# Linear attention into two MLPs: a chunk's y stays on the chip, in 32-partition slots

## Chip, cores and metric

One core of a Trainium2 chip runs the whole program. The metric is device time in microseconds (us), as the median of several executions; engine names are those of the profile: PE (TensorE matmul), PEld (its weight loads), DVE (VectorE), ACT (ScalarE), POOL (GpSimd), SP (the queue that issues the DMAs).

## What is computed

A gated linear attention with 4 batches of 8 heads of 48, over 768 steps, then two MLPs over all 3072 tokens of 384 features (8 heads x 48). Cut to what matters:

```python
for t in range(S):                                    # S = 768, state is (B, H, 48, 48)
    state = alpha[:, :, t, :, None] * state + einsum('bhd,bhe->bhde', k[:, :, t], v[:, :, t])
    y[:, :, t] = einsum('bhd,bhde->bhe', q[:, :, t], state)
x = y.transpose(0, 2, 1, 3).reshape(B * S, H * D)     # 3072 x 384
h = x @ w1_in;  x1 = (h * sigmoid(1.702 * h)) @ w1_out   # 384 -> 2048 -> 384
h = x1 @ w2_in; out = (h - tanh(h)) @ w2_out
```

## The kernel before

**The MLPs.** Tokens go in six blocks of 512 per layer. A step is one block and one of 16 slices of d_ff: `gemm1` (L367) makes 128 rows of h with 9 matmuls 128x128x512, `gemm2` (L376) adds them into three accumulators with 9 more, three steps later (`LAG`). Each factor is split in a high and a low part (`whi`/`wlo`, `xhi`/`xlo`, `ghi`/`glo`), so a product costs three matmuls. The weights come as 64-bit words, and DVE and ACT convert them slice by slice with `conv` (L451: `w_bits`, `w_join`, `w_split`, L159 to L192), during the opening and the first token block.

**The attention.** It goes by chunks of 128 tokens, 24 of them (`g`), six to a batch (`c = g % 6`). Heads are taken in four pairs `p`: a pair's features lie on 112 partitions, head 0 on 0 to 47 and head 1 on 64 to 111. Per chunk: DVE scans the decays (`a_scan`, L241) and scales q and k (`a_scale`, L247 and L248; POOL does that from chunk 8 on). `a_scores` (L270) makes scores for two pairs at a time in banks b and b+1, ACT and POOL (DVE from chunk 8 on) copy and mask them into `sm`, and ACT copies the rest into `kts`. `a_out` (L293) then makes y in banks b and b+1 from two parts: `carried` (L306, 8 matmuls 48x48x128 from `state`, not for c = 0) and the part inside the chunk (L313, 8 matmuls 128x48x128 from v and `sm`); and the chunk's addition to the state (L322, 8 matmuls 128x48x48) in bank 7. `a_state` (L327) updates `state` on DVE (L333, L334, or L336 for c = 0). A matmul of plain fp32 is two instructions on PE in the profile, so 8 matmuls show as x16.

**From y to x.** `a_evac` (L338) copies y from the two banks to `ysb` on ACT (L341) and writes it to the DRAM tensor `xt` in four DMAs (L346). `a_back` (L356) reads it back into `xlo` with features in the order of x, on 128 partitions by 3 (L359). `a_x` (L361) rounds it into `xhi` on ACT (L363) and leaves the rest in `xlo` by a subtraction (L364: DVE for the first 8 chunks, POOL after).

**Order.** Chunks 0 to 3 run in an opening loop (L522 to L548), since the first token block needs all four. Chunks 4 to 7 run inside the steps of the first block, three steps each (`attend`, L484, with its parts r = 0 to 3). Up to the end of the first block every engine keeps the order of the program (`in_order`, L497). Chunks 8 to 23 run inside the steps of blocks 1 to 4, where a planner orders the instructions of each engine. In all places the queues are in order: what stands behind a waiting instruction waits too. In the first block the program has on DVE, per chunk g: `a_scale(g + 1)`, then `a_state(g)`, with three conversions of weights around them, and the first scores of chunk g + 1 (banks 5 and 6) come on PE after `a_out(g)`.

Of the kernel before, what the change touches and what calls it, by code (L numbers as in the profile page):

```python
# [68 lines left out]
def linear_attention_mlps(ctx, tc, xq, xv, fa, fv, cst, w1, w2, out):  # L69
# [30 lines left out]
    state = T("state", (DP, NP, D))  # L100
# [29 lines left out]
    ysb = [carve(NP * C), wtb[:, : NP * C]]  # L130
# [139 lines left out]
    def a_scores(g, x, b):  # L270
        u = (2 * g + x) % 2
# [20 lines left out]

    def a_out(g, b):  # L293
        c = g % NCH
        q = qq(g)
        y = [bank[b + hh][:, : 2 * C].rearrange("p (a t) -> p a t", a=2) for hh in range(2)]
        heads = [(p, hh) for a in range(2) for hh in range(2) for p in (2 * a, 2 * a + 1)]

        def at(p, hh):
            return y[hh][64 * (p % 2) : 64 * (p % 2) + D, p // 2]  # L300

        def carried(start):
            for p in range(NP):
                for hh in range(2):
                    r = slice(64 * hh, 64 * hh + D)
                    P.matmul(out=at(p, hh), lhsT=state[r, p], rhs=q[r, p, :C], start=start and p < 2, stop=not start and p >= 2)  # L306
# [4 lines left out]
        for p, hh in heads:  # L311
            s4 = sm[p // 2].rearrange("p (b a t) -> p b a t", b=2, a=2)
            P.matmul(out=at(p, hh), lhsT=vt(g)[:, p, D * hh : D * hh + D], rhs=s4[:, hh, p % 2],  # L313
                     start=(early or not c) and p < 2, stop=not (c and early) and p >= 2)
        if c and early:
            carried(False)
        if c < NCH - 1:
            dl = bank[7][:DP, : NP * D].rearrange("p (a e) -> p a e", a=NP)
            for p in range(NP):
                for hh in range(2):  # L320
                    kt = kts[p // 2].rearrange("p (b a d) -> p b a d", b=2, a=2)
                    P.matmul(out=dl[64 * hh : 64 * hh + D, p], lhsT=kt[:, hh, p % 2], rhs=vt(g)[:, p, D * hh : D * hh + D],  # L322
                             start=True, stop=True)
            if g >= FULL:
                a_state(g)

    def a_state(g):  # L327
        c = g % NCH
        if c < NCH - 1:
            dl = bank[7][:DP, : NP * D].rearrange("p (a e) -> p a e", a=NP)  # L330
            al = dec3(g + 1, 0)[:, :, C:].to_broadcast([DP, NP, D])
# [6 lines left out]
    def a_evac(g, b):  # L338
        ys = ysb[g % 2 if g < FULL else 0]
        for hh in range(2):  # L340
            A.copy(ys[:DP, 2 * C * hh : 2 * C * hh + 2 * C], bank[b + hh][:DP, : 2 * C])  # L341
        y4 = ys.rearrange("p (b a t) -> p b a t", b=2, a=2)
        tk = slice(g * C, g * C + C)
        for n in range(2):
            for hh in range(2):
                SP.dma_start(out=xt[2 * n + hh :: 4, :, tk].rearrange("h d t -> d h t"), in_=y4[64 * n : 64 * n + D, hh])  # L346
        if g >= FULL:
            a_back(g)
            a_x(g)


# [4 lines left out]
    def a_back(g):  # L356
        _, xl, o = a_at(g)
        tk = slice(g * C, g * C + C)
        SP.dma_start(out=xl[:, :, o].bitcast(F32), in_=xt.rearrange("h d t -> (h d) t")[:, tk].rearrange("(k p) t -> p k t", p=128))  # L359

    def a_x(g):  # L361
        xh, xl, o = a_at(g)
        A.copy(xh[:, :, o], xl[:, :, o].bitcast(F32))  # L363
        (V if g < FULL else G).tensor_tensor(out=xl[:, :, o], in0=xl[:, :, o].bitcast(F32), in1=xh[:, :, o].bitcast(F32), op=ALU.subtract)  # L364
# [112 lines left out]
    def a_done(g, b=5):  # L477
# [3 lines left out]
        if g < FULL:  # L481
            a_back(g)
# [32 lines left out]
    for b in (0, 1, 7):  # L515
        V.memset(bank[b], 0.0)
# [5 lines left out]
    for g in range(4):  # L522
# [12 lines left out]
        if g > 1:  # L535
            a_x(g - 2)
# [7 lines left out]
        if g:  # L544
            a_back(g - 1)
# [3 lines left out]
    a_back(3)  # L549
    conv(1)  # L550
    a_x(2)
# [194 lines left out]
```

## Time and profile before

| | |
|---|---|
| median of 3 runs | 960.14 us (960.0 to 963.54) |
| profiled execution | 956.15 us, of which the span is 954.1 us |
| PE busy | 920.1 us (96%), 4870 matmul instructions |
| DVE busy | 555.7 us (58%) |
| ACT busy | 462.6 us (48%) |
| POOL busy | 187.4 us (20%) |
| chain that ended last | PE 92%, DMA 2%, DVE 2%, ACT 1%, issue 1%, POOL 1% |

The span is cut by stage in what follows: the opening (to 46.5 us), the first steps (to 69 us), the rest of the first token block (to 134.3 us), blocks 1 to 4 with chunks 8 to 23 (to 460 us), and the rest without attention. "Busy" of PE is from records whose ends are modelled, so the distance from one start to the next tells more than the length of a row. A row of the timeline merges equal instructions that follow one another; the count stands at its end, and in square brackets the time that the engine had waited before it and for whom.

### The profile page before, as it was taken

To read this page: it belongs to the slowest core of one execution; us is meant where nothing else is said; L and a number is where in the kernel's file an instruction comes from. 1 tells how busy PE (TensorE), PEld (TensorE's weight loads), DVE (VectorE), ACT (ScalarE), POOL (GpSimd) and SP (SyncE) were. 2 spreads that over 40 slices of the span, in tenths; PEclk is the share of its full clock that TensorE was granted. 3 is DMA by queue.
4 is the path that set the end of the run, shared out by engine and by line. 5 is a ranking of instruction groups with operands and counts; after the bars stand their busy time and mean duration, and the time that the engine had idled before them with its cause. 6 is when DMAs were issued, how large, how long until landed. Compare 5 with 4: busy or idle time off the path is not lost.

```text
span 954.1 us, 13148 instructions
## 1 busy us (share of the span) xinstructions
PE 920.1 (96%) x4870; PEld 726.8 (76%) x4870; DVE 555.7 (58%) x820; ACT 462.6 (48%) x970; POOL 187.4 (20%) x150
## 2 busy tenths in 40 slices
PE   5579999999999999999999999999999999999997
PEld 4457777777777777777788888888888888888885
DVE  7899952231332332622059986766777777766663
ACT  4456534434344544433344564545656566544542
POOL 1101214444344444352400200100101001000000
PEclk9999999999999999999999999999999999999999
DMA  9867423341545534841235410200322430000001
GB/s 264 246 204 239 136 70 107 81 136 37 184 146 187 159 122 138 292 150 50 72 108 169 148 51 1 85 16 1 125 87 87 166 100 0 34 1 1 34 0 38
DMA packets 58041, 101.83 MB, mean 107 GB/s; under 512 B 4992, under 2 KB 37376, under 8 KB 57968
## 3 DMA queue, kind: packets, MB, share of 16 engines
q1 hardware_dynamic: 57968, 100.90, 33.4%
q8 instruction: 40, 0.66, 0.3%
q14 instruction: 33, 0.27, 0.1%
HBM read 86.73 MB, written 14.16 MB: 106 GB/s over the span
## 4 chain that ended last, share of the span: by engine, by line
PE 92%; DMA 2%; DVE 2%; ACT 1%; issue 1%; POOL 1%; SPq 0%; DVEq 0%; POOLq 0%; ACTq 0%
PE bank L380 42%; PE bank L373 41%; PE bank L277 4%; PE bank L313 3%; PE bank L306 1%; PE bank L322 1%; DMA arena<-xq 1%; DMA cs<-cst 1%; POOL arena L287 1%; DVE arena L241 0%; DMA xlo<-xt 0%; DVE wlo L192 0%; ACT whi L191 0%; ACT arena L282 0%; DVE xs L174 0%
## 5 line engine op out<-in xcount | busy, mean ns | idle before, releaser
L373 PE MATMUL bank<-xhi,whi 128*128 128x512 f32 x576 | 229.8, 399 | 8.3 <-ACT xhi L363 8.3
L380 PE MATMUL bank<-ghi,whi 128*128 128x512 f32 x576 | 230.5, 400 | 0.0
L373 PE MATMUL bank<-xlo,whi 128*128 128x512 f32 x576 | 229.6, 399 | 0.0
L373 PE MATMUL bank<-xhi,wlo 128*128 128x512 f32 x576 | 228.8, 397 | 0.0
L380 PE MATMUL bank<-ghi,wlo 128*128 128x512 f32 x576 | 228.1, 396 | 0.0
L380 PE MATMUL bank<-glo,whi 128*128 128x512 f32 x576 | 228.1, 397 | 0.0
L390 ACT CAST ghi<-gt 128x512 fp32r<-128x512 f32 x192 | 119.2, 621 | 186.1 <-DVE gt L402 130.6
L391 DVE TENSOR_TENSOR glo<-gt,ghi 128x512 fp32r<-128x512 f32 x128 | 93.1, 727 | 106.3 <-ACT ghi L390 102.7
L373 PEld LDWEIGHTS bank<-xhi,whi 128*128 128x128 f32 x576 | 109.1, 189 | 35.0 <-ACT xhi L363 8.4
L380 PEld LDWEIGHTS bank<-ghi,whi 128*128 128x128 f32 x576 | 108.7, 189 | 27.5 <-issue 2.9
L373 PEld LDWEIGHTS bank<-xlo,whi 128*128 128x128 f32 x576 | 109.1, 189 | 26.3 <-issue 1.0
L373 PEld LDWEIGHTS bank<-xhi,wlo 128*128 128x128 f32 x576 | 109.2, 190 | 25.4 <-issue 0.4
L380 PEld LDWEIGHTS bank<-glo,whi 128*128 128x128 f32 x576 | 108.7, 189 | 26.0 <-issue 0.8
L380 PEld LDWEIGHTS bank<-ghi,wlo 128*128 128x128 f32 x576 | 108.8, 189 | 24.6 <-issue 0.2
L391 POOL TENSOR_TENSOR glo<-gt,ghi 128x512 fp32r<-128x512 f32 x64 | 86.9, 1358 | 108.1 <-ACT ghi L390 82.4
L241 DVE TENSOR_TENSOR_SCAN arena<-arena,seg 112x516 f32<-112x516 f32 x46 | 66.4, 1444 | 50.3 <-DMA arena<-xq 31.4
L439 POOL TENSOR_TENSOR xlo<-arena,xhi 128x512 fp32r<-128x512 f32 x18 | 27.5, 1555 | 309.5 <-ACT xhi L438 309.5
L387 ACT ACTIVATE gt<-bank 128x512 f32<-128x512 f32 x96 | 57.5, 599 | 61.8 <-PE bank L373 57.2
L400 DVE SCALAR_TENSOR_TENSOR arena<-arena,bank 128x512 f32<-128x512 f32 x96 | 65.8, 685 | 30.1 <-ACT arena L398 29.3
L398 ACT ACTIVATE arena<-bank 128x512 f32<-128x512 f32 x96 | 57.3, 597 | 37.3 <-PE bank L373 36.9
L284 DVE TENSOR_TENSOR arena<-bank,cs 128x256 f32<-128x256 f32 x64 | 24.1, 416 | 86.9 <-PE bank L277 73.8
L402 DVE SCALAR_TENSOR_TENSOR gt<-arena 128x512 f32<-128x512 f32 x96 | 68.3, 712 | 10.2 <-DVE arena L401 0.5
(86 smaller groups left out, 785.3 us busy)
## 6 DMA issues: line engine op xcount, KB each, us to landing
raw<-w SPq DMA_DIRECT2D x64, 768.0 KB, 4.6
arena<-xq SPq DMA_DIRECT2D x46, 224.0 KB, 3.1
arena<-xq SPq DMA_DIRECT2D x22, 451.5 KB, 5.3
xlo<-xt SPq DMA_DIRECT2D x24, 192.0 KB, 4.3
x1t<-xs SPq DMA_DIRECT2D x6, 768.0 KB, 5.0
arena<-x1t SPq DMA_DIRECT2D x6, 768.0 KB, 4.5
out<-xs SPq DMA_DIRECT2D x18, 256.0 KB, 2.3
arena<-xv SPq DMA_DIRECT2D x23, 192.0 KB, 3.2
```

The lines of the kernel that those rows point to most:

```text
L241: V.tensor_tensor_scan(out=dec(g, n), data0=src(g, n), data1=seg, initial=0.0, op0=ALU.mult, op1=ALU.max)
L277: P.matmul(out=o[hh][:, i], lhsT=k[r, 2 * x + i], rhs=q[r, 2 * x + i], start=True, stop=True)
L313: P.matmul(out=at(p, hh), lhsT=vt(g)[:, p, D * hh : D * hh + D], rhs=s4[:, hh, p % 2], start=(early or not c) and p < 2, stop=not (c and e ...
L373: P.matmul(out=h, lhsT=w[m][:, ws], rhs=x[:, k, :n], start=c == 0, stop=c == 3 * KT - 1)
L380: P.matmul(out=acc[k][:, :n], lhsT=w[m][:, ws], rhs=x[s % 3][:, :n], start=m == 0 and c == 0, stop=m == MT - 1 and c == 2)
L387: A.activation(out=gf[i][:, :n], in_=h, func=AF.Silu, scale=1.702)
L390: A.copy(ghi[s % 3][:, :n], gf[s % 2][:, :n])
L391: e.tensor_tensor(out=glo[s % 3][:, :n], in0=gf[s % 2][:, :n], in1=ghi[s % 3][:, :n].bitcast(F32), op=ALU.subtract)
L398: A.activation(out=u, in_=h, func=AF.Square, accum_out=usum[:, s - NS1 :][:, :1])
L400: V.scalar_tensor_tensor(out=p, in0=u, scalar=P3, in1=h, op0=ALU.mult, op1=ALU.mult)
L402: V.scalar_tensor_tensor(out=gf[i], in0=w, scalar=PD, in1=p, op0=ALU.add, op1=ALU.mult)
L439: G.tensor_tensor(out=xlo[i][:, k], in0=xr[:, k], in1=xhi[i][:, k].bitcast(F32), op=ALU.subtract)
```

## The change

y is made where x has it. Features 0 to 383 of x lie in three groups k of 128 partitions; a pair of heads has 96 of them, that is three slots of 32: the first 32 of head 0, a shared slot (its last 16 and the first 16 of head 1), and the last 32 of head 1. Slot j = 3p + n lies in group j // 4 at partitions 32 (j % 4). One bank holds all twelve slots.

`state` becomes block-diagonal, 112 partitions by 96 columns a pair, and bank 7 likewise, set to zero once outside its blocks. `carried` has 12 matmuls of 112x32x128 in place of 8 of 48x48x128; the inner part has 16 of 128x32x128 in place of 8 of 128x48x128, since a shared slot takes one from either head, with v padded by zeros in the new tile `vmid`. `a_mid` fills `vmid` on ACT, two small copies a chunk. `a_state` works on twice as many columns. `a_evac` reads the bank twice, ACT into `xhi` and DVE for the subtraction into `xlo`, for all chunks. The DMAs to and from `xt`, the copies to `ysb`, `a_back` and `a_x` go; so does zeroing banks 0 and 1. The diff:

```diff
-    state = T("state", (DP, NP, D))
+    state = T("state", (DP, NP, 2 * D))
-    ysb = [carve(NP * C), wtb[:, : NP * C]]
+    vmid = [carve(H * 32).rearrange("p (a b e) -> p a b e", a=NP, b=2) for _ in range(2)]
...
     def a_scores(g, x, b):
+        if x == 0:
+            a_mid(g)
...
+    def a_mid(g):
+        v = src(g, 4).rearrange("p (a d) -> p a d", a=NP)[:, :, 32:64].rearrange("p a (b e) -> p a b e", b=2)
+        for hh in range(2):
+            A.copy(vmid[g % 2][:, :, hh, 16 * hh : 16 * hh + 16], v[:, :, hh])
+
     def a_out(g, b):
         c = g % NCH
         q = qq(g)
-        y = [bank[b + hh][:, : 2 * C].rearrange("p (a t) -> p a t", a=2) for hh in range(2)]
-        heads = [(p, hh) for a in range(2) for hh in range(2) for p in (2 * a, 2 * a + 1)]
-
-        def at(p, hh):
-            return y[hh][64 * (p % 2) : 64 * (p % 2) + D, p // 2]
+        y = bank[b][:, : KT * C].rearrange("p (k t) -> p k t", k=KT)
+        slots = [(k, [(j // 3, j % 3) for j in range(4 * k, 4 * k + 4)]) for k in range(KT)]
+
+        def at(p, n):
+            j = 3 * p + n
+            return y[32 * (j % 4) : 32 * (j % 4) + 32, j // 4]
 
         def carried(start):
-            for p in range(NP):
-                for hh in range(2):
-                    r = slice(64 * hh, 64 * hh + D)
-                    P.matmul(out=at(p, hh), lhsT=state[r, p], rhs=q[r, p, :C], start=start and p < 2, stop=not start and p >= 2)
+            for k, ps in slots:
+                for p, n in ps:
+                    P.matmul(out=at(p, n), lhsT=state[:, p, 32 * n : 32 * n + 32], rhs=q[:, p, :C],
+                             start=start and not k, stop=not start and k == 2)
+
+        def inner(start):
+            for k, ps in slots:
+                for p, n, hh in [(p, n, n // 2) for p, n in ps] + [(p, n, 1) for p, n in ps if n == 1]:
+                    s4 = sm[p // 2].rearrange("p (b a t) -> p b a t", b=2, a=2)
+                    w = vmid[g % 2][:, p, hh] if n == 1 else vt(g)[:, p, 32 * n : 32 * n + 32]
+                    P.matmul(out=at(p, n), lhsT=w, rhs=s4[:, hh, p % 2], start=start and not k and (n != 1 or not hh),
+                             stop=not (c and early) and k == 2 and (n != 1 or hh == 1))
 
         early = g < L1[0][1] // C
         if c and not early:
             carried(True)
-        for p, hh in heads:
-            s4 = sm[p // 2].rearrange("p (b a t) -> p b a t", b=2, a=2)
-            P.matmul(out=at(p, hh), lhsT=vt(g)[:, p, D * hh : D * hh + D], rhs=s4[:, hh, p % 2],
-                     start=(early or not c) and p < 2, stop=not (c and early) and p >= 2)
+        inner(early or not c)
         if c and early:
             carried(False)
...
-                    P.matmul(out=dl[64 * hh : 64 * hh + D, p], lhsT=kt[:, hh, p % 2], rhs=vt(g)[:, p, D * hh : D * hh + D],
-                             start=True, stop=True)
+                    r = slice(D * hh, D * hh + D)
+                    P.matmul(out=dl[64 * hh : 64 * hh + D, p, r], lhsT=kt[:, hh, p % 2], rhs=vt(g)[:, p, r], start=True, stop=True)
...
-            dl = bank[7][:DP, : NP * D].rearrange("p (a e) -> p a e", a=NP)
-            al = dec3(g + 1, 0)[:, :, C:].to_broadcast([DP, NP, D])
+            dl = bank[7][:DP, : 2 * NP * D].rearrange("p (a e) -> p a e", a=NP)
+            al = dec3(g + 1, 0)[:, :, C:].to_broadcast([DP, NP, 2 * D])
...
-    def a_evac(g, b):
-        ys = ysb[g % 2 if g < FULL else 0]
-        for hh in range(2):
-            A.copy(ys[:DP, 2 * C * hh : 2 * C * hh + 2 * C], bank[b + hh][:DP, : 2 * C])
...
-    def a_back(g):
...
-    def a_x(g):
+    def a_evac(g, b):
         xh, xl, o = a_at(g)
-        A.copy(xh[:, :, o], xl[:, :, o].bitcast(F32))
-        (V if g < FULL else G).tensor_tensor(out=xl[:, :, o], in0=xl[:, :, o].bitcast(F32), in1=xh[:, :, o].bitcast(F32), op=ALU.subtract)
+        y = bank[b][:, : KT * C].rearrange("p (k t) -> p k t", k=KT)
+        A.copy(xh[:, :, o], y)
+        V.tensor_tensor(out=xl[:, :, o], in0=y, in1=xh[:, :, o].bitcast(F32), op=ALU.subtract)
...
-    for b in (0, 1, 7):
-        V.memset(bank[b], 0.0)
+    V.memset(bank[7], 0.0)
+    for t in vmid:
+        G.memset(t, 0.0)
...
-        if g > 1:
-            a_x(g - 2)
...
-        if g:
-            a_back(g - 1)
...
-    a_back(3)
     conv(1)
-    a_x(2)
-    a_x(3)
...
-                if m % 3 == 1 and m > 3:
-                    a_x(m // 3 + 3)
```

## Rows read from the trace of the kernel before

**Rows 1.** The page: busy shares, and PE and DVE in 40 slices

```profile
PE 920.1 (96%) x4870; PEld 726.8 (76%) x4870; DVE 555.7 (58%) x820; ACT 462.6 (48%) x970; POOL 187.4 (20%) x150
...
PE   5579999999999999999999999999999999999997
...
DVE  7899952231332332622059986766777777766663
```

**Rows 2.** Windows by stage: us, busy of PE, PEld, DVE, ACT, POOL, clock, DMA, GB/s

```profile
46.40:69.00 22.60, 16.56 (x100) 11.79 (x100) 20.21 (x28) 11.77 (x25) 1.63 (x2) 1.00 0.67 198
69.00:134.30 65.30, 65.25 (x385) 50.90 (x386) 60.64 (x82) 34.00 (x76) 12.02 (x10) 0.97 0.58 176
134.30:460.00 325.70, 325.08 (x2047) 250.13 (x2046) 97.42 (x174) 136.96 (x304) 131.69 (x104) 1.00 0.42 131
```

**Rows 3.** Timeline, end of the opening: start us, us, engine line, count, [idle before]

```profile
36.30 1.11 PE L306 MATMUL bank<-arena,state 48*48 48x128 f32 x16
...
41.50 0.38 SPq L359 DMA_DIRECT2D xlo<-xt  x1
...
45.92 0.51 ACT L363 CAST xhi<-xlo 128x384 fp32r<-128x384 f32 x1 [2.75 <-DMA xlo<-xt]
...
46.47 0.56 DVE L364 TENSOR_TENSOR xlo<-xlo,xhi 128x384 fp32r<-128x384 f32 x1 [2.29 <-ACT xhi L363]
...
46.49 0.79 PE L373 MATMUL bank<-xhi,whi 128*128 128x512 f32 x1 [8.27 <-ACT xhi L363]
```

**Rows 4.** Timeline of DVE: its other longer waits between 20 and 69 us

```profile
22.83 0.36 DVE L333 TENSOR_TENSOR state<-bank,state 112x192 f32<-112x192 f32 x1 [1.04 <-PE bank L322]
...
32.47 0.96 DVE L192 TENSOR_TENSOR wlo<-cf,whi 128x768 fp32r<-128x768 f32 x1 [0.76 <-ACT whi L191]
...
53.64 0.96 DVE L192 TENSOR_TENSOR wlo<-xs,whi 128x768 fp32r<-128x768 f32 x1 [1.94 <-ACT whi L191]
```

**Rows 5.** Timeline: scores of chunks 5 and 7, and DVE's scaling before them

```profile
68.26 0.68 DVE L248 TENSOR_TENSOR arena<-arena 112x512 f32<-112x512 f32 x1
...
69.05 1.51 PE L277 MATMUL bank<-arena 48*128 48x176 f32 x8 [5.11 <-issue]
...
101.84 0.68 DVE L248 TENSOR_TENSOR arena<-arena 112x512 f32<-112x512 f32 x1
...
103.06 0.87 PE L277 MATMUL bank<-arena 48*128 48x176 f32 x8
```

**Rows 6.** Timeline of PE in very short windows: how many passes have started

```profile
59.62 0.33 PE L306 MATMUL bank<-arena,state 48*48 48x128 f32 x4
...
60.21 0.32 PE L313 MATMUL bank<-arena 128*48 128x128 f32 x2
...
251.35 0.42 PE L306 MATMUL bank<-arena,state 48*48 48x128 f32 x2 [0.58 <-ACT arena L290]
...
251.50 0.51 PE L306 MATMUL bank<-arena,state 48*48 48x128 f32 x5
```

**Rows 7.** Timeline of PE: carried and inner part of one later chunk

```profile
59.62 0.65 PE L306 MATMUL bank<-arena,state 48*48 48x128 f32 x16
60.21 1.08 PE L313 MATMUL bank<-arena 128*48 128x128 f32 x16
```

**Rows 8.** Groups by form: busy us, mean ns of one, idle before

```profile
L284 DVE TENSOR_TENSOR arena<-bank,cs 128x256 f32<-128x256 f32 x64 | 24.1, 416 | 86.9 <-PE bank L277 73.8 <-issue 8.8 <-ACT gt L387 4.0
...
L290 ACT COPY arena<-bank 128x96 f32<-128x96 f32 x96 | 21.6, 247 | 68.2 <-DVE arena L284 65.8
...
L333 DVE TENSOR_TENSOR state<-bank,state 112x192 f32<-112x192 f32 x16 | 5.7, 355 | 32.3 <-PE bank L322 32.3
...
L364 DVE TENSOR_TENSOR xlo<-xlo,xhi 128x384 fp32r<-128x384 f32 x8 | 4.3, 540 | 2.3 <-ACT xhi L363 2.3
```

**Rows 9.** Timeline of PE in the middle stage: end of a chunk, next scores

```profile
150.06 0.35 PE L322 MATMUL bank<-arena 128*48 128x48 f32 x8
...
154.72 0.87 PE L277 MATMUL bank<-arena 48*128 48x176 f32 x8
```

More of the change, by code (lines that the diff above doesn't have):

```diff
@@ L329, in a_state @@
         if c < NCH - 1:
-            dl = bank[7][:DP, : NP * D].rearrange("p (a e) -> p a e", a=NP)
-            al = dec3(g + 1, 0)[:, :, C:].to_broadcast([DP, NP, D])
+            dl = bank[7][:DP, : 2 * NP * D].rearrange("p (a e) -> p a e", a=NP)
+            al = dec3(g + 1, 0)[:, :, C:].to_broadcast([DP, NP, 2 * D])
             if c:
@@ L336, in a_state @@
                 V.tensor_tensor(out=state, in0=dl, in1=al, op=ALU.mult)
-    def a_evac(g, b):
-        ys = ysb[g % 2 if g < FULL else 0]
-        for hh in range(2):
-            A.copy(ys[:DP, 2 * C * hh : 2 * C * hh + 2 * C], bank[b + hh][:DP, : 2 * C])
[L342 to L349, printed above, removed]
     def a_at(g):
@@ L354, in a_at @@
         return xhi[j % 2], xlo[j % 2], slice(g * C - L1[j][0], g * C - L1[j][0] + C)
-    def a_back(g):
-        _, xl, o = a_at(g)
-        tk = slice(g * C, g * C + C)
-        SP.dma_start(out=xl[:, :, o].bitcast(F32), in_=xt.rearrange("h d t -> (h d) t")[:, tk].rearrange("(k p) t -> p k t", p=128))
-    def a_x(g):
+    def a_evac(g, b):
         xh, xl, o = a_at(g)
-        A.copy(xh[:, :, o], xl[:, :, o].bitcast(F32))
-        (V if g < FULL else G).tensor_tensor(out=xl[:, :, o], in0=xl[:, :, o].bitcast(F32), in1=xh[:, :, o].bitcast(F32), op=ALU.subtract)
+        y = bank[b][:, : KT * C].rearrange("p (k t) -> p k t", k=KT)
+        A.copy(xh[:, :, o], y)
+        V.tensor_tensor(out=xl[:, :, o], in0=y, in1=xh[:, :, o].bitcast(F32), op=ALU.subtract)
     def gemm1(i, m, h, n):
@@ L480, in a_done @@
             a_load(g + 2)
-        if g < FULL:
-            a_back(g)
     def attend(g, r, b=5):
```

## The prediction, made before the changed kernel was run

> **What bounds the kernel now.** I read the page's busy shares and its 40 slices first: PE is busy 96% and its digits are 9 from the fourth slice on, while DVE's are 7, 8 and then three times 9, that is up to 119 us, and low after them [rows 1]. The windows by stage say the same more sharply. From 69 to 134 us PE is busy 65.25 of 65.30 us and from 134 to 460 us 325.08 of 325.70, so there every PE instruction that is added lengthens the run by its own length. From 46.4 to 69 us it is different: PE is busy 16.56 of 22.60 us, DVE 20.21 [rows 2]. So there are two questions: what the change does to the path that ends at 69 us, and what it adds on PE after that.
>
> The round trip of y is seen at the end of the opening. PE's last carried part starts at 36.30, the read back from DRAM is issued at 41.50, ACT has waited 2.75 us when it rounds that chunk at 45.92, DVE has waited 2.29, and PE has stood still 8.27 us when the first gemm1 starts at 46.49 [rows 3]. That looks like 8 us to be had. But PE stops again, for 5.11 us, before the scores of chunk 5 at 69.05, and what it waits for is DVE's scaling that begins at 68.26 and lasts 0.68 [rows 5]. Between the two DVE waited once, 1.94 us [rows 4]. What PE gains at 46.49 it therefore loses again at 69.05, unless DVE's chain gets shorter. I cost the opening on DVE, not on PE.
>
> **PE, the size of a pass.** An fp32 matmul shows as two passes. At 251.35 the first head's matmul runs alone, because the next one waits for a bank: its two passes are the only two started until the window's end at 251.67; then, in the next 0.05 us, four passes of other heads start [rows 6]. So passes of one place in the array go one after another, and passes at different places go side by side, and a later matmul overtakes the waiting second pass of an earlier one. How many go abreast follows the shape: 48x48 (four places) starts four within 0.03 us, 128x48 (two places) starts two [rows 6]. The sixteen inner passes fill 60.21 to 61.12 less the hand-over, eight groups in 0.91, that is 0.114 us a group; the sixteen carried ones are four groups, 0.46, and 0.13 of the 0.59 to the next line is the switch to another shape [rows 7].
>
> The new matmuls have 32 columns and all rows, so four places. *Carried*: 12 matmuls, 24 passes, six groups in place of four: +0.23 us a chunk. *Inner*: 16 matmuls, 32 passes, eight groups if always four abreast, as many as now: +0. But its order isn't regular: the second matmul of a shared slot follows at once, and one place then gets two in turn while others wait. If a waiting matmul holds back all behind it, I count five rounds in place of four, ten groups: +0.23 us. I take eight, since [rows 6] show waiting passes overtaken, and keep ten for the range. The switch between carried and inner goes, one between inner and the state's part (L322) comes: nothing net.
>
> Here a rule of the Trainium skill speaks against the change. "TensorE: Matmul & The Clock Gate", Part 3, The mechanism, says that matmuls start and end strictly in program order. The trace disagrees for different places of the array: four carried passes within 0.03 us [rows 6] can't be in the order first, second, first, second. What it would cost if it came true is the third case below.
>
> **PE after 69 us.** Chunks 5 to 23 lie there; 16 of them have a carried part (6, 12 and 18 don't): 16 x 0.23 = +3.7 us, and the inner part 19 x (0 to 0.23) = 0 to +4.4. Chunk 4 falls into the stop before 69.05 and costs nothing as long as that stop is there.
>
> **DVE up to 69 us**, step by step, where + is later. In the opening a pass takes about twice as long: sixteen carried passes last 1.11 us at 36.30 and 0.65 at 59.62 [rows 3, 7]. Carried thus costs 0.46 a chunk, less about 0.2 for a switch that goes since L306 and L313 now share a shape: chunks 1 and 2 bring DVE's update of the state after chunk 2 +0.5, as it waits for PE (the like wait of chunk 1 is 1.04 in [rows 4]). The update handles 384 columns in place of 192: from 355 ns for 192 and 416 for 256 columns [rows 8], about 1 ns a column, I estimate 0.54, so +0.18 an operation and +0.36 a chunk. The subtraction for x now follows at once, from PSUM; SBUF took 540 ns for the same 384 columns, the slope above gives the same: 0.55. So after chunk 2: +0.5 +0.36 +0.55. The 0.76 wait that comes next [rows 4] is filled by that, and the subtraction of chunk 1, which stood before chunk 3's update, is gone (-0.54): about +0.1. Chunk 3's update and subtraction: +0.36 +0.55, so +1.0. Then what stood between the conversions goes: two subtractions and the 2.29 wait [rows 3], -3.4: DVE is 2.4 us early. The 1.94 wait stays: it comes from ACT's guard behind the scaling, and both only move. At the scaling of chunk 5 DVE is still 2.4 early, but then chunk 4's subtraction stands between it and the scores, which write the bank it reads: +0.55. PE resumes 1.8 us earlier. With ten groups chunks 0 to 2 cost 0.46 more each, 1.4 together, and 0.4 is left. What is late next is the same chain, DVE's conversions.
>
> After that DVE must keep up until the first block ends: before chunk 7's scores the scaling ends 0.54 us early (101.84 + 0.68 against 103.06) [rows 5]. DVE has 2.4 of gain and about 0.9 of new work (one update, one subtraction more), PE 1.8 of gain and 0.23 of new work: it still holds, barely.
>
> **What lies beside other work.** ACT loses two copies and one rounding that waits for a DMA, and gets one rounding from PSUM and two short copies, each at most like the 247 ns for 96 columns [rows 8]; ACT was busy 48% [rows 1]. POOL loses 16 subtractions and DVE gets them in a stage where it is busy 97 of 326 us [rows 2]. SP loses five DMAs a chunk, so loads behind them start earlier; no wait that PE feels hung on them. The new wait on PE in the middle stage is bank 5: next scores wait for ACT's rounding and then DVE's subtraction. From the end of a chunk at about 150.06 to the next scores at 154.72 there are 4.7 us [rows 9], and the two need 0.5 + 0.55 and at most one instruction ahead on each engine. I cost it at 0; if DVE is then held in a scan that waits for its load, PE stops behind it, with all that is queued: up to 1.5 us over the run for the range.
>
> **Sum.** -1.8 + 3.7 = +1.9 us on the profiled execution: 958.0. That execution is 956.15 (span 954.1), 3.99 below the median of 960.14. So the forecast is 962.0, by itself 959.5 to 964.5.
>
> **Rivals.**
> 1. *Ten groups in the inner part*, on PE. -0.4 + 3.7 + 4.4 = +7.7, so 967.8. For it: nothing in the trace shows an irregular order, and a waiting matmul may hold back those behind it. Against it: the overtaking in [rows 6]. It takes the time past 0.5% from the point where one of the two groups a chunk is lost: 19 x 0.114 = 2.2 and 0.7 at the start, +4.8 in all.
> 2. *Only two abreast*, the place is PE again: if four moving streams through all rows don't go, or order is strict. Carried 12 groups for 4 and inner 16 for 8, +0.91 each: 16 x 1.82 + 3 x 0.91 = 31.9, and about 7 in the opening: 999. Against it: four abreast is shown for two places by two, though with 48 of 128 rows each. By the page's rule on order named above it is this case.
> 3. *DVE doesn't hold the first steps*: then the 8.27 and the 5.11 both go [rows 3, 5], less 0.8 for the opening's passes: -13.4 + 0.8 + 3.7 = -8.9, so 951.2. Against it: DVE busy 20.21 of 22.60 us [rows 2].
> That the change doesn't do what it says (the DMAs stay, or the wait) I see no way for.
>
> **Chances.** Forecast 50%, ten groups 34%, two abreast 6%, rival 3 5%, and 5% for a new order of the planner in the middle stage, worth 1 or 2 us either way. The range goes from the forecast's own low end less 1 to rival 1 plus the stops of bank 5: 958.5 to 969.5. A difference over 0.5% (4.8 us) is about what a measurement of this kernel can tell from no change: below 955.3 only rival 3, 5%; above 964.9 most of ten groups, two abreast and a little of the forecast, 42%; the rest, 53%, within.
>
> **What would show it.** Carried as x24 over about 0.68 us and inner as x32 over 0.91 (right) or 1.14 (rival 1), and four starts within 0.03 us; a first gemm1 some 4 us earlier, but a longer stop before chunk 5's scores, ended by DVE's subtraction at 66.5 to 69; PE without stops after it. I would be wrong if that stop has gone, if scores wait at bank 5 in the middle stage, or if the carried and inner groups together take over 2.5 us.

## The result and the profile after

The changed kernel takes 972.52 us (median of 4 runs, 972.0 to 973.65), the kernel before 960.11 beside it: ratio 1.0131, 95% interval 1.0114 to 1.0149. That is slower by 12.4 us, outside the range of 958.5 to 969.5. The profiled execution of after took 972.51 (span 970.8), which is its median; that of before took 956.15, 4 us under its own. So between the two traces there are 16.4 us, and they are what the rows below have to explain.

The page of after, busy shares and the 40 slices of PE and DVE (against [rows 1]), and the windows by stage with the columns of [rows 2]:

```profile
PE 932.0 (96%) x5414; PEld 733.6 (76%) x5414; DVE 568.4 (59%) x834; ACT 455.0 (47%) x970; POOL 172.7 (18%) x136
...
PE   4479999999999999999999999999999999999997
...
DVE  7999852331242332632039986766777777766663
```

```profile
46.40:69.00 22.60, 13.27 (x119) 10.07 (x121) 20.41 (x29) 11.41 (x26) 2.03 (x2) 0.83 0.74 233
69.00:134.00 65.00, 65.00 (x441) 50.50 (x440) 58.39 (x78) 32.28 (x76) 11.46 (x10) 0.96 0.50 145
134.00:460.00 326.00, 326.00 (x2310) 250.59 (x2309) 108.61 (x186) 127.85 (x291) 112.50 (x86) 1.00 0.35 112
```

The shares tell nothing: PE 96% before, 96% after. The clock column of the first window needs care: before shows 1.00 there [rows 2] and after 0.83, but the trace of before has no clock record ahead of 55.5 us, and up to then its gemm1 matmuls start 0.43 us apart, behind that 0.23. In the windows PE is busy without a gap from 69 to 460 us. So the time isn't in a wait; PE has more to do, or does it more slowly. How much, and where, the ends of the blocks tell. DVE copies one third of each finished block of tokens out of PSUM; here the first of these twelve copies, the fifth (the last block that has attention beside it) and the last, first before, then after (timeline of DVE):

```profile
148.68 0.69 DVE L423 TENSOR_SCALAR xs<-bank 128x512 f32<-128x512 f32 x1 [4.36 <-PE bank L380]
...
483.80 0.69 DVE L423 TENSOR_SCALAR xs<-bank 128x512 f32<-128x512 f32 x1 [2.26 <-PE bank L380]
...
947.15 0.69 DVE L423 TENSOR_SCALAR xs<-bank 128x512 f32<-128x512 f32 x1 [1.90 <-PE bank L380]
```

```profile
149.80 0.69 DVE L421 TENSOR_SCALAR xs<-bank 128x512 f32<-128x512 f32 x1 [4.35 <-PE bank L378]
...
498.68 0.69 DVE L421 TENSOR_SCALAR xs<-bank 128x512 f32<-128x512 f32 x1 [2.28 <-PE bank L378]
...
963.90 0.69 DVE L421 TENSOR_SCALAR xs<-bank 128x512 f32<-128x512 f32 x1 [1.91 <-PE bank L378]
```

After is 1.1 us late at the first, 14.9 at the fifth and 16.75 at the last. The loss arises between 150 and 500 us, where the attention of the later chunks is slipped between the matmuls of the first MLP, and 1.9 us come in the seven blocks behind it, which hold no attention and which the change doesn't touch. The timeline of PE in that stage shows what it is (against [rows 7, 9]); the first fence is before and holds the start that follows the scores of [rows 9], the second is after, the third ACT and DVE of after beside it:

```profile
155.52 0.50 PE L373 MATMUL bank<-xhi,whi 128*128 128x512 f32 x1
```

```profile
149.70 0.86 PE L315 MATMUL bank<-arena,state 112*32 112x128 f32 x24
150.38 1.08 PE L323 MATMUL bank<-arena 128*32 128x128 f32 x32
151.39 0.39 PE L338 MATMUL bank<-arena 128*48 128x48 f32 x8
151.70 0.86 PE L280 MATMUL bank<-arena 48*128 48x176 f32 x4
152.50 0.50 PE L378 MATMUL bank<-ghi,whi 128*128 128x512 f32 x1
...
157.58 0.86 PE L280 MATMUL bank<-arena 48*128 48x176 f32 x4
158.37 0.50 PE L371 MATMUL bank<-xhi,whi 128*128 128x512 f32 x1
...
160.44 0.86 PE L280 MATMUL bank<-arena 48*128 48x176 f32 x4
161.23 0.50 PE L371 MATMUL bank<-xhi,wlo 128*128 128x512 f32 x1
```

```profile
151.52 0.48 ACT L361 CAST xhi<-bank 128x384 fp32r<-128x384 f32 x1 [1.82 <-PE bank L323]
...
152.30 0.55 DVE L362 TENSOR_TENSOR xlo<-bank,xhi 128x384 fp32r<-128x384 f32 x1
```

The new matmuls go as forecast: carried, 24 passes, 0.68 us to the next line; inner, 32 passes, 1.01. But the scores (L280), which the change doesn't touch, now stand as **x4** where [rows 9] have **x8**, and four passes take as long as eight: 151.70 to 152.50, 0.80 us; 157.58 to 158.37, 0.79; in the kernel before, 154.72 to 155.52 with eight, 0.80. A group of scores is four matmuls, two into bank 5 (heads in partitions 0 to 47) and two into bank 6 (partitions 64 to 111). When the four follow each other, one of each bank goes side by side: in the kernel before the passes from 154.72 on start in twos (154.72, 154.73; 154.98, 154.98), in the changed kernel one by one (151.70, 151.96, 152.11, 152.26). The planner now issues the two of one bank apart from the two of the other, with other matmuls between them, and two of the same partitions go one after the other. That the half at 151.70 is bank 6's follows from ACT and DVE, which read y out of bank 5 until 152.85.

Counted in the trace after 75 us, where there are 37 groups (a sum is the time from the first start of a group to the next matmul of another kind):

| us on PE after 75 us | before | after |
|---|---|---|
| scores | 31.2 | 41.8 |
| whole groups, halved (4+4), cut (2+6) | 34, 1, 2 | 21, 15, 1 |
| carried, inner, dl | 10.0, 17.7, 8.6 | 10.9, 19.3, 9.2 |
| changes from MLP to attention matmuls | 59 | 65 |

Scores +10.6 us (14 more halved groups at 0.79 more are 11.1, one cut less about -0.5), carried, inner and dl +3.0, six more changes of shape at about 0.1 on the way in and 0.1 on the way out (0.33 and 0.34 to the next start in place of 0.23) +1.2, less the stop of 0.58 at 251.35 that only the kernel before has [rows 6], and what the opening leaves, +0.6 at the second score group of chunk 5 (76.43 for 75.80): 14.8 of the 14.9 at the fifth copy.

The end of the opening (against [rows 3 to 5]), timeline of after, and behind it the scores of chunk 4 in the kernel before:

```profile
41.05 0.49 PE L371 MATMUL bank<-xhi,whi 128*128 128x512 f32 x1
...
50.41 1.54 PE L280 MATMUL bank<-arena 48*128 48x176 f32 x8 [5.48 <-DVE arena L249]
...
52.30 0.96 DVE L193 TENSOR_TENSOR wlo<-xs,whi 128x768 fp32r<-128x768 f32 x1 [1.94 <-ACT whi L192]
...
67.04 0.68 DVE L249 TENSOR_TENSOR arena<-arena 112x512 f32<-112x512 f32 x1
...
67.64 0.55 DVE L362 TENSOR_TENSOR xlo<-bank,xhi 128x384 fp32r<-128x384 f32 x1
...
68.25 1.54 PE L280 MATMUL bank<-arena 48*128 48x176 f32 x8 [5.32 <-DVE xlo L362]
```

```profile
51.75 1.54 PE L277 MATMUL bank<-arena 48*128 48x176 f32 x8 [0.89 <-DVE arena L248]
```

The first gemm1 starts 5.4 us earlier, and PE loses most of it already before chunk 4's scores: there it stands for 5.48 us in place of 0.89, until DVE's scaling is done, and starts only 1.3 us earlier (50.41 for 51.75). Before chunk 5's scores it stands for 5.32 us in place of 5.11, until DVE's scaling and then its subtraction for x are done; 0.8 us is left. Behind that stop the granted clock is at the lower level (1.2 of 2.4 GHz) for 6.8 us; in the kernel before it was for 3.4. Windows of after, then of before, the columns as above:

```profile
68.00:74.80 6.80, 6.55 (x20) 5.11 (x21) 6.65 (x12) 3.81 (x9) 1.31 (x1) 0.50 0.94 277
```

```profile
69.10:72.50 3.40, 3.40 (x13) 2.63 (x14) 3.33 (x6) 1.93 (x6) 0.97 (x1) 0.50 1.05 336
```

That is why the 0.8 us that PE is early at 68.25 are 0.6 late at 76.43.

### The profile page after: what moved, and what is told of

It is laid out like the page before. It is cut to its first block, busy times and chain, and to the rows that moved or that the text cites. A ratio compares the mean times of both kernels' runs of the same rounds, so it can differ in the third digit from the quotient of the medians.

```text
span 970.8 us, 14011 instructions
## 1 busy us (share of the span) xinstructions
PE 932.0 (96%) x5414; PEld 733.6 (76%) x5414; DVE 568.4 (59%) x834; ACT 455.0 (47%) x970; POOL 172.7 (18%) x136
## 4 chain that ended last, share of the span: by engine, by line
PE 93%; DVE 4%; DMA 1%; issue 1%; POOL 0%; ACT 0%; SPq 0%; ACTq 0%; POOLq 0%
PE bank L378 42%; PE bank L371 41%; PE bank L280 5%; PE bank L323 2%; PE bank L315 1%; PE bank L338 1%; DMA arena<-xv 1%; DVE wlo L193 0%; POOL arena L290 0%; DVE arena L242 0%; DVE cf L175 0%; DVE cf L162 0%; DVE cf L163 0%; DVE xlo L362 0%; DVE xs L163 0%
## 5 line engine op out<-in xcount | busy, mean ns | idle before, releaser
L385 ACT ACTIVATE gt<-bank 128x512 f32<-128x512 f32 x96 | 57.8, 602 | 74.7 <-PE bank L371 66.5
L242 DVE TENSOR_TENSOR_SCAN arena<-arena,seg 112x516 f32<-112x516 f32 x46 | 64.4, 1401 | 38.2 <-DMA arena<-xq 36.3
L280 PE MATMUL bank<-arena 48*128 48x176 f32 x368 | 55.5, 351 | 22.8 <-DVE arena L249 8.8
```

The lines of the kernel that those rows point to most:

```text
L242: V.tensor_tensor_scan(out=dec(g, n), data0=src(g, n), data1=seg, initial=0.0, op0=ALU.mult, op1=ALU.max)
L280: P.matmul(out=o[hh][:, i], lhsT=k[r, 2 * x + i], rhs=q[r, 2 * x + i], start=True, stop=True)
L385: A.activation(out=gf[i][:, :n], in_=h, func=AF.Silu, scale=1.702)
```

## The experiments

Two theories were to be told apart for the 10.6 us: the scores cost more because they stand apart (A), or the larger state, the new dependences and the new places of y cost it in some way that the scores only show (B). Beside that stood the prediction's reading of the opening, that DVE sets the end of the stop. All ratios are against the kernel before on the same chip.

| run | whole, halved, cut | scores us | median us | ratio, 95% interval |
|---|---|---|---|---|
| after | 21, 15, 1 | 41.8 | 972.52 | 1.0131 (1.0114 to 1.0149) |
| e1_pairs | 28, 0, 8 | 33.3 | 966.54 | 1.0074 (1.0045 to 1.0103) |
| e5_line | 31, 0, 6 | 32.6 | 963.32 | 1.0047 (1.0022 to 1.0072) |
| e6_scan_late | 32, 0, 5 | 31.9 | 961.47 | 1.0019 (1.0004 to 1.0034) |
| e10_two_banks | 30, 7, 0 | 35.1 | 965.78 | 1.0056 (1.0034 to 1.0078) |
| e2_before_banks | 30, 7, 0 | 35.2 | 963.22 | 1.0028 (1.0013 to 1.0043) |
| e12_before_held | 32, 1, 4 | 31.9 | 962.31 | 1.0014 (0.9995 to 1.0033) |

(One or two groups are missing from some traces.)

### The four score matmuls kept together

```diff
+        last = None
         for i in range(2):
             for hh in range(2):
-                P.matmul(out=o[hh][:, i], ...)
+                mm = P.matmul(out=o[hh][:, i], ...)
+                if last is not None:
+                    tc.add_manual_dep(mm.ins, last.ins.name, NoSync, reason="pairs")
+                last = mm
```

> The changed kernel, with the four score matmuls of two pairs chained in issue order (bank 5, 6, 5, 6), so that the planner can't issue bank 6's two alone. Theory A (split scores): in the changed kernel 30 halves of score groups stand alone and take 0.79 us each, as long as a whole group (0.80), so 15 groups cost 0.79 more and a switch of shape more. Whole again, scores fall from 41.8 us to about 31 and the run to 960 to 962. Theory B (bank 5): the planner only filled a wait for DVE's subtraction on bank 5; with the chain PE stops there instead and the run stays at 968 to 972. Theory C (the new 32-column matmuls or the clock): scores don't matter, 971 to 973.

Measured: 966.54, between the times of A (960 to 962) and B (968 to 972); 6.0 of the 12.4 us are back with an edit that only orders instructions on PE. The scores fell by 8.5 us, which the larger state and the new dependences can't give, as they are still there. But more than the 0.79 of a half hides in the rest: eight groups are still cut after the first matmul, dl is cut five times (11.15 us for 9.18), and there is a new stop. Timeline of DVE and PE of e1_pairs:

```profile
419.85 2.24 DVE L242 TENSOR_TENSOR_SCAN arena<-arena,seg 112x516 f32<-112x516 f32 x1 [8.99 <-DMA arena<-xq]
422.12 0.18 DVE L244 RECIPROCAL seg<-arena 112x4 f32<-112x4 f32 x1
422.22 0.39 DVE L292 TENSOR_TENSOR arena<-bank,cs 128x256 f32<-128x256 f32 x1
```

```profile
420.82 0.39 PE L383 MATMUL bank<-ghi,wlo 128*128 128x512 f32 x1
422.94 0.56 PE L281 MATMUL bank<-arena 48*128 48x176 f32 x2 [1.73 <-ACT arena L298]
423.43 0.29 PE L343 MATMUL bank<-arena 128*48 128x48 f32 x2
424.39 1.54 PE L281 MATMUL bank<-arena 48*128 48x176 f32 x6 [0.67 <-ACT arena L298]
```

```profile
424.10:431.00 6.90, 6.61 (x23) 5.18 (x24) 0.85 (x2) 2.35 (x6) 3.44 (x3) 0.51 0.12 33
```

DVE waits 8.99 us for the load of its next scan; the mask (L292) is queued behind that scan, though its scores had been made from 415.04 on, ACT's copy stands behind the mask, the next scores behind the copy. PE stops for 1.73 and 0.67 us, and then the granted clock is 0.51 for 6.9 us. The prediction had named such a stop, DVE "held in a scan that waits for its load", at up to 1.5 us, but with the subtraction for x held by it; here that was done at 410.39 and it is the mask.

### The price of a half, in the kernel before

```diff
-        for i in range(2):
-            for hh in range(2):
+        last = None
+        for hh in range(2):
+            for i in range(2):
```

The matmuls are chained as in e1_pairs, but in the order bank 5, 5, 6, 6.

> The kernel before, with the scores' order changed alone: both matmuls of bank 5, then both of bank 6, chained. Theory A, if a waiting pass is overtaken by one at another place: groups that stay together still take 0.80 us, those which the planner parts by other work cost 0.6 to 0.8 more each; 960 to 968 by how many are parted. If nothing is overtaken, the passes of one bank go one after another and every group takes about 1.4 us: 38 x 0.6 = 23 more, 983. Theories B and C: 960 (nothing but order is changed).

Timeline of PE:

```profile
154.95 0.87 PE L278 MATMUL bank<-arena 48*128 48x176 f32 x8
155.75 0.50 PE L385 MATMUL bank<-ghi,whi 128*128 128x512 f32 x1
...
160.61 0.86 PE L278 MATMUL bank<-arena 48*128 48x176 f32 x4
161.40 0.29 PE L327 MATMUL bank<-arena 128*48 128x48 f32 x2
161.62 0.86 PE L278 MATMUL bank<-arena 48*128 48x176 f32 x4
162.41 0.38 PE L327 MATMUL bank<-arena 128*48 128x48 f32 x6
```

As long as the four stand together the order does no harm: the group at 154.95 still takes 0.80 us, so the matmuls of bank 6 overtake the waiting second one of bank 5. Only where the planner put other work between the halves, seven times, do they cost 0.79 each: scores +4.0 us. With nothing of the change in it, the kernel before gets slower, by 3.4 us in the medians and 2.7 by the ratio. Not all of that need be the parting: dl is cut six times here too (9.9 us for 8.6), and this trace has the slower of two paces in the blocks without attention (last section).

The Trainium skill says the same from the other side ("TensorE: Matmul & The Clock Gate", section Why this matters for your kernels): small-K matmuls run concurrently when each lands in a distinct row group. The trace agrees: two of one bank share their partitions, 0.40 us each; one of each bank, 0.20 each.

### All attention matmuls in program order, and the scan behind the masks

e5_line: every matmul of scores, carried, inner and dl is chained behind the one before it; the MLP's may still come between. e6_scan_late: the same, and

```diff
+        if g > FULL:
+            tc.add_manual_dep(sc.ins, masked[0], NoSync, reason="scan")
...
-        if r == 0:
-            prep(g + 1, 0)
         if r < 2:
             a_scores(g, r, b)
+        if r == 0:
+            prep(g + 1, 0)
```

> Change: the kernel after, with all of PE's attention matmuls (scores, carried, inner, dl) held in program order among themselves, scores in the order bank 5, 6, 5, 6. Then neither dl nor the other half stands between the two banks' scores; 6 of about 38 groups are still parted by a gemm, one matmul from three. Theory A (the loss is scores that stand apart): the scores after 75 us fall from 41.8 us to about 32.5 and dl from 9.2 to about 8, so against the kernel after 10 to 11 us less on PE; if the stop near 420 us that the version with paired scores had comes again, 965 to 967, and without it 960 to 962. Rival B (the scores' order isn't what costs, the larger state and the new dependences do): no less than the 966.5 of the version with paired scores, whatever scores and dl sum to.

> Change: the kernel of the run e5_line, and DVE's first scan of a chunk from chunk 9 on stands behind the masks of the chunk before it. Theory: the stop near 420 us in the version with paired scores is masks that stand behind a scan which waits for its load; then no PE wait for ACT's copies and no low granted clock lies between 415 and 432 us, and the time is 4 to 6 us under a kernel that has that stop: 960 to 962. Rival: the scan only comes later and the scaling behind it becomes what PE waits for: the stop moves a few us, the clock falls as before, 965 to 967.

Measured: 963.32 and 961.47. e5_line has the stop near 420 again, shorter (2.11 us, then a clock of 0.50 for 3.4 us), and lies between the two times expected. In e6_scan_late it is gone; the windows of the same stretch:

```profile
415.00:424.00 9.00, 8.73 (x40) 6.44 (x39) 2.70 (x6) 3.28 (x10) 3.90 (x4) 1.00 0.43 128
424.00:432.00 8.00, 8.00 (x98) 6.40 (x97) 1.49 (x3) 3.63 (x8) 2.44 (x2) 1.00 0.21 55
```

PE is busy 16.73 of 17 us and the clock is 1.00; a stop of 0.74 us comes at 409.24, where PE waits for DVE's copy of a finished block, without a fall of the clock. The gain over e5_line, 1.9 us, is less than the 4 to 6 that were expected: e5_line's stop was the short one, and in the two profiled executions e6_scan_late has the slower of the two paces (1.9 us, last section). With whole scores and without the stop the changed kernel is at 961.5, and 11 of the 12.4 us are accounted for by two orders of instructions. That this is near the forecast (962.0) is in part luck: 1.8 us of it come from dl in one piece (7.4 us for 9.2), which the forecast didn't have.

### The held order in the kernel before

> Change: the kernel before, with all of PE's attention matmuls held in program order among themselves, scores in the order bank 6, 5, 6, 5 (35 of 41 score groups of four then stand whole, as 37 of 41 in the kernel before). A control: what the held order itself does. Theory A: the kernel before loses nothing in its scores, so there is nothing to regain: 957 to 963. Rival: the held order is good in itself (fewer switches, dl in one piece): 1 to 3 us less, and then the gain of e5_line against the kernel after is in part that.

> Change: the kernel before, with PE's attention matmuls held in program order among themselves, and from chunk 5 on the scores in the order bank 6, 5, 6, 5; the opening has the order of the kernel before (in e7_before_line it had not). 35 of 41 score groups stand whole. It is the control for e6_scan_late: what the held order is worth without the change. Theory A (the held order only mends the parted scores, and the kernel before has almost none): 958 to 961.5, with dl in one piece about 1.5 us less on PE, so that the changed kernel with whole scores stands 0 to 3.5 us behind. Rival (holding the order costs, by waits that PE then stands in): 962 to 965, and the change itself would be worth more than e6_scan_late shows.

e7_before_line gave 962.38 (1.0030, 1.0004 to 1.0057). It had the other order of banks in the opening too, where the first gemm1 then started at 49.87 (before: 46.49), so it isn't a clean control. e12_before_held has the opening's order of before: 962.31, 1.0014 (0.9995 to 1.0033). Its first gemm1 started at 48.82 all the same, so most of that delay is there without the other order, and its profiled execution (964.21) carries 2.3 us of it. The held order brings the kernel before nothing: dl takes 1.8 us less, but a stop arises that wasn't there (timeline of PE):

```profile
342.85 1.11 PE L273 MATMUL bank<-arena,state 48*48 48x128 f32 x16 [3.62 <-ACT arena L299]
```

with 6.8 us of half clock from 341.5 on. Both expectations are met by half: 962.3 is the rival's time, and holding the order does cost a wait. So whether the change with whole scores is level with the kernel before or a microsecond or two behind or ahead stays open; e6_scan_late (1.0019) and e12_before_held (1.0014) are not told apart.

### Why the planner parts them

```diff
-        y = bank[b][:, : KT * C].rearrange("p (k t) -> p k t", k=KT)
+        y = [bank[b + (k == 2 and b == 5)][:, k * C : k * C + C] for k in range(KT)]
```

> Change: the kernel after, with y's third part of 128 rows in bank 6 and the first two in bank 5, from chunk 4 on; nothing is held in order by hand. Banks 5 and 6 then come free about together, as in the kernel before. In the order of the instructions 14 halves of a score group stand apart in place of 30, and 5 dl groups are cut. Theory (the new place of y is why the planner parts the scores): scores after 75 us at 34.5 to 36, 6 to 7 us less on PE than in the kernel after, dl about 1.5 more, one rounding and one subtraction more a chunk beside it: 966 to 968. Rival (the parting comes from elsewhere or costs nothing): 971 to 974.

Measured: 965.78, scores 35.1 us. With y's third part back in bank 6, and nothing ordered by hand, 7 groups are halved in place of 15, and 6.7 us of the run are back, as much as the scores lost. (In the profiled executions other things cancel beside it: dl +1.1, a stop of 1.96 us at 345.05, and the faster pace of the last section, -1.9.) So the new place of y, all in bank 5, is why at least half of them part: bank 6 comes free earlier than bank 5 (151.70 against 152.85 above). That the planner issues whatever it finds ready is inferred. Where the other seven come from (the kernel before has one) stays open.

### Who ends the stop in the opening

e8_less_dve leaves one bit operation of DVE out of five weight slices; e9_no_lo and e11_scan_no_lo leave out the subtraction for the low part of five slices:

```diff
-        V.tensor_tensor(out=wlo[m], in0=f, in1=whi[m].bitcast(F32), op=ALU.subtract)
+        if l == 2 or not 0 < m < 6:
+            V.tensor_tensor(out=wlo[m], in0=f, in1=whi[m].bitcast(F32), op=ALU.subtract)
```

> Change: the kernel after, without the second of the two bit operations of DVE that open a weight slice, for slices 1 to 5 of the first layer (0.95 us each; the signs of these weights are left out). Theory: DVE sets the end of the opening's second stop, so chunk 5's scores come 3.5 to 4.8 us earlier than 68.25, and the run is 3 to 5 us shorter (967.5 to 969.5). Rival: DVE waits for others in that stretch (loads of weight slices, ACT's guard), and less than 1.5 us of it arrives: 971 to 973.

> Change: the kernel after, without DVE's subtraction for the low part of the weights (0.95 us each) of slices 1 to 5 of the first layer; their matmuls read the low part of another slice, so PE's work is the same and only a small term of the result differs. Theory: DVE sets the end of the opening's second stop, so chunk 5's scores come 3.5 to 4.8 us earlier than 68.25, and the run is 3 to 5 us shorter (967.5 to 969.5). Rival: DVE waits for others in that stretch (loads of weight slices, ACT's guard), and less than 1.5 us of it arrives: 971 to 973.

> Change: the kernel of the run e6_scan_late, with the same subtractions of slices 1 to 5 left out as in e9_no_lo. It prices the opening's stop where nothing else stops PE. Theory (the stop is DVE's and its end moves the whole rest): 3.5 to 5 us under e6_scan_late, 956.5 to 958. Rival (PE then waits for a load or the clock falls for longer): within 2 us of it, 959.5 to 962.

The time of e8_less_dve (12055 us) says nothing: without the signs the kernel's own flag sent the program through its second, slow branch as well. Its opening can be read: chunk 5's scores start at 64.42, 3.8 us earlier. e9_no_lo, timeline and the window behind the stop:

```profile
62.72 0.55 DVE L365 TENSOR_TENSOR xlo<-bank,xhi 128x384 fp32r<-128x384 f32 x1
...
63.33 0.87 PE L283 MATMUL bank<-arena 48*128 48x176 f32 x8 [1.43 <-DVE xlo L365]
```

```profile
60.00:80.00 20.00, 18.41 (x135) 13.81 (x133) 19.75 (x29) 10.46 (x26) 3.04 (x2) 1.00 0.66 204
```

4.8 us of DVE less, and the scores come 4.9 earlier; the stop is 1.43 us in place of 5.32, the clock stays at 1.00, and the run is 966.77, 5.75 shorter. e11_scan_no_lo does the same on e6_scan_late: 955.64 (0.9958, 0.9939 to 0.9977), 5.8 shorter. The stop is DVE's, and the run gets shorter with it, but not one for one: without the half clock behind the stop the second score group of chunk 5 comes 7.9 us earlier in e9_no_lo (68.50 for 76.43), and two new stops, 0.97 us at 80.81 (for DVE's subtraction) and 0.73 at 103.10, take part of it back. e11_scan_no_lo is 0.4% under the kernel before, but at the price of part of the result; no run here takes that work off DVE and keeps the result.

The obvious way was tried on e1_pairs, the same five subtractions on POOL, and a second edit that moves ACT's two short copies behind the first score copies:

```diff
-    V.tensor_tensor(out=wlo[m], in0=f, in1=whi[m].bitcast(F32), op=ALU.subtract)
+    (G if l == 1 and 0 < m < 6 else V).tensor_tensor(out=wlo[m], in0=f, ...)
```

> As e1_pairs, with the subtraction of w_split on POOL in place of DVE for slices 1 to 5 of layer 1. Theory (DVE's chain sets the first steps): five times 0.95 us leave DVE before the scores of chunk 5, which come 3.5 to 4.7 us earlier than in e1_pairs, and the run is 3 to 5 us below e1_pairs. Rival: PE's own order or POOL sets the stop; then it ends where it did, and the run is within 1 us of e1_pairs or above it (POOL took 1.36 us for 512 columns where DVE took 0.73).

> As e1_pairs, with the copies into vmid behind the first scores' copies on ACT, not ahead of them. In the changed kernel the first inner matmul starts at 13.46 us, before it was 11.89. Theory: ACT stands at vmid's copy until v has landed, and the scores' copies, the mask and PE behind it; moved, DVE's first state update comes about 1.2 us earlier (from 16.85) and the scores of chunk 5 0.5 to 1.2 earlier: 0.5 to 1.2 below e1_pairs. Rival: the mask on POOL or PE's passes set it, and nothing moves.

e4_pool_split: 969.41, slower than e1_pairs by 2.9. Timeline:

```profile
42.53 1.80 POOL L193 TENSOR_TENSOR wlo<-cf,whi 128x768 fp32r<-128x768 f32 x1 [4.17 <-ACT whi L192]
42.64 2.10 DVE L354 TENSOR_TENSOR state<-state,arena 112x384 f32<-112x384 f32 x1
...
47.02 2.19 POOL L193 TENSOR_TENSOR wlo<-cf,whi 128x768 fp32r<-128x768 f32 x1 [2.69 <-ACT whi L192]
47.58 2.46 DVE L175 SCALAR_TENSOR_TENSOR xs<-raw,xs 128x768 int32<-128x768 int32 x1
```

The state's second operation takes 2.10 us beside POOL's subtraction and 0.56 alone, the join 2.46 for 0.95. DVE got nothing back, chunk 5's scores came at 70.49 (66.94 in e1_pairs). The Trainium skill names it ("Advanced Engine Details and Errata", Miscellaneous Facts, GPSIMD Details): GpSimd shares a read and a write interface with VectorE and conflicts with VectorE instructions that have two SBUF inputs. These rows agree: both DVE instructions read two operands from SBUF. e3_mid_late: 966.56, chunk 5's scores at 66.90, no gain in sum. But its first inner matmuls started 0.7 us earlier than in e1_pairs (11.68 for 12.37) and DVE's first update 0.4 (15.34 for 15.76), although the load for DVE's scan of chunk 1 came 0.8 later (9.96 for 9.17); DVE then waited 0.47 us for PE at the second update, where e1_pairs has no wait. What these copies cost with equal loads isn't shown.

## Why the prediction was wrong

**The step that failed** is "5% for a new order of the planner in the middle stage, worth 1 or 2 us either way". The order changed, and it was worth 10.6 us. The prediction weighed the new wait on bank 5 only as a wait ("I cost it at 0", with a stop of up to 1.5 us). It didn't ask what the planner does when the two banks of a score group no longer come free together. It could be read beside [rows 9]: eight passes of 48 rows took 0.80 us (154.72 to 155.52), and the change's own matmuls were costed by exactly that rule, that passes at different places go side by side. The scores were not costed at all, since the diff doesn't touch them.

**Right: the size of a pass.** Carried x24 in 0.68, inner x32 in 1.01 with a change of shape in it. Carried, inner and dl together came to +3.0 us (0.9, 1.6 and 0.6 by line, as a change of shape that stood behind carried now stands behind inner); the forecast had +3.7. So rivals 1 (ten groups, +7.7 in all) and 2 (two abreast, 999) fell: four carried passes start within 0.02 us (149.70 to 149.72), and in e2_before_banks whole groups in the order 5, 5, 6, 6 are as fast as in 5, 6, 5, 6. The Trainium skill's rule on strict order, which the prediction cites, doesn't fit these rows.

**Right: the opening is DVE's.** PE's gain of 5.4 us at the first gemm1 was lost again, 4.1 of it before chunk 4's scores and 0.5 more before chunk 5's, and e8, e9 and e11 show that DVE's work sets that end. Rival 3 fell. The subtraction at 0.55 and the state's operations at 0.56 were as estimated (0.55, 0.54), and the 1.94 wait stayed.

**The size of the opening's gain** was put at 1.8 us; the two profiled executions show 0.8. DVE's chain shows where the difference arises: at the conversion behind chunk 3's subtraction it is 2.2 us late (42.67 for 40.43), where the sum had 1.0; the 3.4 us that it then had to gain came (3.6). One wait was put at nothing: on ACT the copies into `vmid` stand ahead of chunk 0's scores' copies and wait 0.46 us for v, so that the first inner matmuls start at 13.46 for 11.89 and DVE's first update at 16.85 for 15.19. How much of the difference that is can't be told from these executions: the same opening ends at 66.90, 66.94, 68.25, 68.53, 68.62 and 68.82 in the six profiled kernels that have the change and all of DVE's work on DVE, and at 69.05, 69.05 and 71.40 in the three with the old opening. DVE's scan of chunk 1 waits for its load until 9.17 (e1_pairs) or 10.26 (after); a later scan is not always a later end, as the two at 69.05 had it at 9.22 and 10.18.

**Not costed: the clock.** 6.8 us at half clock behind the stop for 3.4 before, about 1.4 us: the nine matmuls of gemm2 after those scores take 4.01 us for 3.13 and the next nine 2.69 for 2.19.

**The offset.** The sum was made on an execution of 956.15 and raised by 3.99 to the median. The execution of after had no such offset. So the sum was 14.5 us short between the two traces (+1.9 for +16.4) and 10.5 in the medians. Term by term: scores 10.6, opening with its clock 2.4 (+0.6 for -1.8), blocks without attention 1.9, changes of shape less the stop at 251.35 0.6, passes -0.7: 14.8, with 0.3 of rounding and overlap.

Of the signs listed at the end of the prediction the good ones came true (x24 and x32, an earlier gemm1, a stop ended by DVE's subtraction between 66.5 and 69, PE without stops behind it), but for the longer stop before chunk 5's scores: that one grew by 0.2 us, and the long new one stands before chunk 4's. None of the bad ones came true. They looked at the edited instructions alone; the row that lost the time was not among them.

## What to carry to other kernels

When an edit moves an output to another bank, ask what else uses both banks, whether it was fast because its instructions stood together, and whether the planner will still find them ready together; in a row, look at the count (x8 or x4) before the duration. Where PE is busy all the time a loss shows in no wait and no share: compare the start of the same late instructions in both traces, find the stage where they drift apart, then sum PE there by line. A reordering that costs can be undone, at least in part, by an order edge alone, which also makes it a cheap test of that cause; the edge can bring stops of its own.

## What the hardware showed unexpectedly

- Half a group costs as much as a whole one: 4 passes 0.79 us, 8 passes 0.80.
- A short stop costs more than itself: stops of 2.1 to 5.3 us of PE were followed by 3.4 or 6.8 us at a granted clock of 0.5; where the stop was 1.43 us (e9_no_lo), 1.80 (e11_scan_no_lo, at 403.30) or 1.96 (e10_two_banks, at 345.05) the clock stayed at 1.00. Two stops close together, 1.03 and 0.67 us (e4_pool_split, ended at 425.90 and 427.36), were followed by 3.4 us at 0.5. Nothing was run that varies the stop alone.
- Beside POOL's subtraction two DVE instructions took 2.10 us for 0.56 and 2.46 for 0.95 (e4_pool_split).
- The seven blocks without attention, the same code in all these kernels, take one of two paces: the mean distance of two matmuls there is 232.4 ns (before, e1_pairs, e3_mid_late, e4_pool_split, e5_line, e7_before_line, e10_two_banks, e11_scan_no_lo, e12_before_held) or 233.3 (after, e2_before_banks, e6_scan_late, e9_no_lo). Over 2016 matmuls that is the 1.9 us above. Each kernel has one profiled execution, so whether the pace goes with the kernel or with the execution is open, and so is what it does to the medians.
